# Five groups' second products in seven parts instead of eight, and planned steps handed out twice per block

## The chip, the cores and the metric

The kernel runs on one core of a Trainium2 chip. A core has TensorE (PE in the rows; PEld is its weight load), VectorE (DVE), ScalarE (ACT), GpSimd (POOL) and SyncE (SP, whose queue issues transfers), and 16 DMA engines. The metric is the device time of one execution in microseconds; the time of a kernel is the median of its runs.

## The reference

With x of 2048 rows by 512 columns, and six vectors of 512 from `silu(c) @ w_mod`:

```
h = layernorm(x) * (1 + ca) + sa
x = x + ga * Real(DFT_seq(DFT_hidden(h)))
h = layernorm(x) * (1 + cb) + sb
x = x + gb * ((silu(h @ w1) * (h @ w3)) @ w2)
```

w1 and w3 are 512 x 1792, w2 is 1792 x 512, all in float32. This case is about the last line.

## The kernel before

**Precision.** Every factor of a product is kept as a high part (a rounded copy, made by ScalarE's `copy`) and a low part (what is left, made by VectorE's `minus`). `product` (its matmuls are on L100) issues three matmuls: high by high, high by low, low by high. A matmul is 128 x 128 by 128 x 512. In the rows `hf` holds the two parts of the hidden values, `w2h` and `w2l` those of a weight, and `w1s`, `w1sh`, `w1sl` sums of weight blocks and their parts.

**Tiles.** The 1792 hidden columns are 7 groups g of 2 x 128, the 2048 rows are 4 blocks t of 512, the 512 columns are 4 blocks d of 128. Buffers are 50 slots of 128 x 2 x 512 float32; `take` and `give` hand them out in turn. Results of a matmul go to 8 banks.

**First groups.** `up(0, 0)`, `up(1, 0)`, eight units `down` for t = 0, then `up(0, 2)`, `up(1, 2)`. `up` runs four blocks (`up_block`) of twelve matmuls: w1 and w3, for q = 0 and 1. Blocks rotate over banks 0 to 3, `down` over banks 4 to 7. Rows of t = 2 (`h2h`, `h2l`) come from the layer norm of that block, which is a list of small steps (`ln2`, `chunk_parts`).

**Later groups.** For `items`, first the groups 2 to 6 of pair 0 (t = 0, 2) and then the groups 0 to 6 of pair 1 (t = 1, 3), the first products are made in Strassen's form: seven units `factor` in place of eight, written a1 to a7 for w1 and b1 to b7 for w3, each six matmuls. After most of them VectorE adds the bank to an earlier one (`plus`, L93) and, for w3, multiplies by the silu (`times`, L96); the others are copied by ScalarE. The order is written out by hand: a head `-b7 a1 a2 -b4 -b3` (a minus means the group before) and a body `a6 a5 y a7 y y a4 y a3 y b1 y b2 y b6 b5 y`. A `y` is one `down_unit` of the group before: six matmuls into one of banks 6 and 7 in turn, for one t and one d; ScalarE scales the bank into half a `y` tile (L335), and after two units GpSimd's queue adds the tile to `sums` in DRAM (L1146). Eight units serve one group. For the last two groups of pair 1, VectorE adds the bank to rows in SBUF instead.

**Steps handed out.** Work that prepares later operands stands in two lists: `background` (layer norm steps) and `jobs` (weights: high parts, for w1 and w3 also sums of blocks in four small operations, low parts, high and low parts of the sums). After each unit `beside` credits VectorE and ScalarE with the unit's length less what the unit itself uses of them, and `advance` issues steps from a list while there is credit. A step may push the credit below zero; then its engine must earn it back. A pause in the list ends a call. `jobs` go first; once they are empty the credit is cut to 1.0 and `background` goes on. `drain` issues whatever is still missing when a unit needs it. Each engine executes its instructions in the order in which they were issued. `behind(n, fn)` puts a step at the start of the n-th unit from there, ahead of that unit's own steps; `delayed` runs them.

Of the kernel before, what the change touches and what calls it, by code (L numbers as in the profile page):

```python
# [15 lines left out]
P = 128  # L16
# [26 lines left out]
def folded(nc, pools, c, cp, wmr, wmc, x, xt, ctr, cti, wdr, wdi, w1, w3, w2, out):  # L43
# [42 lines left out]
    def copy(dst, src, scale=1.0):  # L86
        nc.scalar.activation(dst, src, AF.Copy, scale=scale)  # L87

    def minus(dst, a, b):
        nc.vector.tensor_tensor(out=dst, in0=a, in1=b, op=OP.subtract)  # L90
# [4 lines left out]
    def times(dst, a, b):  # L95
        nc.vector.tensor_tensor(out=dst, in0=a, in1=b, op=OP.mult)  # L96
# [966 lines left out]
    def behind(units, fn):  # L1063
        if units:
            later.setdefault(units, []).append(fn)
        else:
            fn()
# [5 lines left out]
            later[n - 1] = later.pop(n)  # L1073


    def up_block(g, t, q, w):
        if q == 0 and w == "w1":
            drain(lambda: ("h2", t, 1) in done)
        to = bank(turn[0] % 4)
        turn[0] += 1  # L1080
        for d in range(ND):
            at = slice(d * P, (d + 1) * P)
            product(
                to,
                [u[:, q, at] for u in wuse[w, g]],
                [u[t, d // 2][:, d % 2, :] for u in (h2h, h2l)],
                d == 0,
                d == ND - 1,
            )
        if t == PAIRS[0][1] and q == 1:  # L1090
            give_w((w, g))
        if w == "w1":
            cur["v"] = take(F32, "v")
            nc.scalar.activation(cur["v"][:, 0, :], to, AF.Silu)
        else:
            v = cur.pop("v")
            times(v[:, 1, :], v[:, 0, :], to)
            u = hf[g, t, q] = take(F32R, "hf")
            copy(u[:, 0, :], v[:, 1, :])
            behind(1, lambda: minus(u[:, 1, :], v[:, 1, :], u[:, 0, :].bitcast(F32)))  # L1100
            behind(1, lambda: give(v))
# [106 lines left out]
    TO = {1: 0, 6: 0, 7: 0, 4: 0, 2: 1, 5: 2, 3: 2}  # L1208
    state, vs = {}, {}

    def right(pair, n):
        t0, t1 = PAIRS[pair]
        if n in (1, 2, 3):
            at = {1: (t0, 0), 2: (t0, 1), 3: (t1, 1)}[n]
            return h2h[at], h2l[at]
        at = pair, {5: 1, 6: 2, 7: 3, 4: 4}[n]
        return th[at], tl[at]

    def result(i, w, q, k, src):

        g, pair = items[i]
        v = vs[i][q][:, k, :]
        if w == "w1":
            behind(k != 0 or q == 0, lambda: nc.scalar.activation(v, src, AF.Silu))  # L1224
            return
        times(v, v, src)

        def highs():
            hf[g, PAIRS[pair][k], q] = take(F32R, "hf")
            copy(hf[g, PAIRS[pair][k], q][:, 0, :], v)  # L1230

        def lows():
            u = hf[g, PAIRS[pair][k], q]
            minus(u[:, 1, :], v, u[:, 0, :].bitcast(F32))

        behind(1, highs)
        behind(2, lows)

    def factor(i, w, n):
        g, pair = items[i]  # L1240
        key = (w, g, pair)
        st = state.setdefault((i, w), {})
        new = n in (1, 2, 5)
        if new:
            st[TO[n]] = bank(TO[n] + (0 if w == "w1" else 3))
        to = st[TO[n]]
        names = ("h", "l") if LEFT[n][0] == "h" else ("sh", "sl")
        for d in range(2):
            at = slice(int(LEFT[n][1]) * HALF + d * P, int(LEFT[n][1]) * HALF + (d + 1) * P)
            product(  # L1250
                to,
                [flat(wuse[key][x])[:, at] for x in names],
                [x[:, d, :] for x in right(pair, n)],
                new and d == 0,
                d == 1,
                not new,
            )
        if n == 1:
            st["x"] = take(F32, "x")
            if w == "w1":  # L1260
                vs[i] = [take(F32, "v") for _ in range(2)]
        if n == 5:
            st["y"] = take(F32, "x")
        if n in (1, 5, 6):
            copy(st["y" if n == 5 else "x"][:, n // 6, :], to)
        elif n == 4:
            result(i, w, 1, 0, to)
        else:

            own = st["y" if n == 7 else "x"][:, n % 2 if n < 7 else 0, :]  # L1270
            q, k = {2: (0, 0), 3: (0, 1), 7: (1, 1)}[n]
            dst = vs[i][q][:, k, :] if w == "w1" else own
            plus(dst, to, own)
            result(i, w, q, k, dst)
            if n == 7:
                behind(1, lambda: give(st["y"]))
        if n == 3:
            for x in wuse.pop(key).values():
                give(x)
            behind(1, lambda: give(st["x"]))  # L1280
            if w == "w3":
                for x in vs.pop(i):
                    behind(3, lambda x=x: give(x))


    loads.extend((n, m) for n in range(len(steps)) for m in range(2))
# [277 lines left out]
    FACTOR["b"].update({6: (0.0, 0.5), 7: (1.8, 0.5)})  # L1564

    def beside(us, used):
        advance(us - used[0], us - used[1], jobs)
        if not jobs:
            advance(0.0, 0.0)

    def up(g, t):
        for q in range(2):
            for w in ("w1", "w3"):
                drain(lambda: ((w, g), "l") in done, jobs)
                delayed()
                up_block(g, t, q, w)
                beside(2.72, USED[w])

    def down(g, pair, t, d, key):
        drain(lambda: (key, "l") in done, jobs)  # L1580
        delayed()
        down_unit(g, pair, t, d, key)
        beside(1.36, USED["own" if pair == 1 and g >= NG - 2 else "y"])

    for w in ("w1", "w3"):
# [35 lines left out]
    def unit(kind, i, n):  # L1621
        g, pair = items[i]
        more = i + 1 < len(items)
        if n == 1:
            drain(lambda: ("ready", i, "w1" if kind == "a" else "w3") in done, jobs)
        if (kind, i, n) == ("a", 0, 6):
            drain(lambda: ("t", 0, 4) in done)
        if (kind, i, n) == ("a", turning, 1):
            drain(lambda: not background)
        if kind == "a" and i == turning and n in (4, 5, 6, 7):  # L1630
            drain(lambda: ("t", 1, {6: 2, 5: 1, 7: 3, 4: 4}[n]) in done, jobs)
        delayed()
        factor(i, "w1" if kind == "a" else "w3", n)
        if (kind, n) == ("a", 1) and more:
            load_w(("w1", *items[i + 1]))
        if (kind, n) == ("a", 6):
            load_w(("w2", g, pair))
        if (kind, n) == ("a", 3) and more:
            load_w(("w3", *items[i + 1]))
            weight_jobs(i + 1, "w1")  # L1640
        if (kind, n) == ("b", 2):
            plain_jobs(("w2", g, pair))
        if (kind, n) == ("b", 3):
            if i + 2 == turning:
# [8 lines left out]
            for t in PAIRS[pair]:  # L1653
                seconds.extend((g, pair, t, d, ("w2", g, pair)) for d in range(ND))
        beside(1.36, FACTOR[kind][n])

    weight_jobs(0, "w3")
# [1 line left out]
    ln2(3)  # L1659
    for i in range(len(items)):  # L1660
        body = "a6 a5 y a7 y y a4 y a3 y b1 y b2 y b6 b5 y"
        if i == turning:
            body = "y y y y y a6 y a5 y a7 y b1 b2 a4 b6 a3 b5"
        if i == len(items) - 1:
            body = "a6 a5 y a7 y y a4 y a3 b1 y b2 b6 b5 y b7 y b4 y b3 y y y y y y y y"
        head = "-b7 a1 -b4 -b3 a2 " if i == turning else "-b7 a1 a2 -b4 -b3 " if i else "a1 a2 "
        for at in (head + body).split():
            if at == "y":
                if (i, len(seconds)) == (len(items) - 1, 4):
                    tc.mark_branch_hint_location("general", hint="LikelyTaken")  # L1670
# [809 lines left out]
```

## Time and profile before

| | |
|---|---|
| median of 3 runs | 707.81 us (705.94 to 708.52) |
| the profiled execution | 708.46 us, its span 706.7 us |
| mean granted TensorE clock | 0.991 |
| DMA traffic | 108.93 MB, mean 154 GB/s |
| accumulations `sum<-y` | 48 of 512 KB, 5.6 us from issue to landing |
| groups of pair 1 | from about 500 us to the end |

A row of the time order has its start and its duration in us, engine, line, operation, what it writes and reads, how many were merged, and in brackets the idle time before it and what ended that. Durations of neighbours on one engine overlap a little, so what a step costs in a full queue is the distance of two starts. A row of the windows has the stretch, its length, the busy time of each engine (with instructions), the granted clock, the share of the DMA engines, and GB/s.

### The profile page before, as it was taken

What the parts mean: (1) busy time and instruction counts of PE and PEld (TensorE: products, weight loads), DVE (VectorE), ACT (ScalarE), POOL (GpSimd) and SP (SyncE); (2) the same over time, 40 slices, a digit from 0 to 9 for tenths busy, and PEclk for the clock granted to TensorE, in tenths of its full rate; (3) what the DMA queues carried; (4) which work ended last, traced back from release to release, by engine and by line L of the source; (5) the groups of instructions that cost most, each with busy time, mean ns of one, the idle gap of its engine ahead of it and who ended that gap; (6) DMA issues with size and microseconds to landing.
All of it is one profiled execution on the core that took longest, in us unless ns stands there. A gap on an engine that the chain in (4) does not pass through costs nothing.

```text
span 706.7 us, 8912 instructions
## 1 busy us (share of the span) xinstructions
PE 686.3 (97%) x3152; PEld 564.7 (80%) x3152; DVE 548.3 (78%) x877; ACT 430.8 (61%) x709; POOL 119.4 (17%) x141
## 2 busy tenths in 40 slices
PE   7999999999999999899999999999999999999995
PEld 4898888888888888687888788787788888888784
DVE  5999679997999978579987886896865556664763
ACT  4998865545454655745677676867665565656420
POOL 1320253542524000200100101011010100101000
PEclk9999999999999999999999999999999999999998
DMA  8730299796678521522868558376763847537403
GB/s 266 211 120 1 77 373 328 251 307 229 207 283 287 168 86 41 92 58 64 209 114 199 89 130 153 61 156 137 239 136 73 180 62 175 111 69 162 137 0 124
DMA packets 38100, 108.93 MB, mean 154 GB/s; under 512 B 4896, under 2 KB 5152, under 8 KB 38048
## 3 DMA queue, kind: packets, MB, share of 16 engines
q0 software_dynamic: 12352, 43.00, 29.3%
q1 hardware_dynamic: 25264, 63.98, 27.5%
q10 hardware_dynamic: 432, 1.31, 0.5%
q8 instruction: 26, 0.43, 0.3%
q14 instruction: 26, 0.21, 0.1%
HBM read 76.81 MB, written 33.55 MB: 156 GB/s over the span
## 4 chain that ended last, share of the span: by engine, by line
PE 81%; DVE 7%; ACT 6%; issue 2%; DMA 2%; SPq 1%; ACTq 0%; DVEq 0%
PE bank L100 52%; PE bank L750 25%; PE bank L559 2%; PE bank L598 1%; DMA wmr<-in_wmr 1%; ACT xc L894 1%; PE bank L576 1%; DVE xc L96 1%; SPq L231 1%; ACT hf L87 1%; ACT y L335 1%; DVE v L96 0%; DVE hl L90 0%; ACT hm L501 0%; DMA w<-in_wdi 0%
## 5 line engine op out<-in xcount | busy, mean ns | idle before, releaser
L100 PE MATMUL bank<-hf,w2h 128*128 128x512 f32 (+1 forms) x452 | 140.9, 391 | 0.3
L1146 POOL DMA_DIRECT2D sum<-y x48 | 41.0, 855 | 390.1 <-ACT y L335 373.0
L100 PEld LDWEIGHTS bank<-hf,w2h 128*128 128x128 f32 x452 | 84.3, 188 | 22.1 <-DVE hf L90 3.4
L100 PE MATMUL bank<-hf,w2l 128*128 128x512 f32 (+1 forms) x226 | 87.6, 388 | 0.0
L87 ACT ACTIVATE hf<-v 128x512 fp32r<-128x512 f32 x56 | 35.3, 630 | 67.3 <-DVE v L96 62.7
L335 ACT ACTIVATE y<-bank,gb 128x512 f32<-128x512 f32 x96 | 64.9, 682 | 18.6 <-PE bank L100 18.3
L93 DVE TENSOR_TENSOR v<-bank,x 128x512 f32<-128x512 f32 x36 | 24.7, 685 | 34.9 <-PE bank L100 34.8
L750 PE MATMUL bank<-bh,us 128*128 128x512 f32 x128 | 49.9, 390 | 0.0
L93 DVE TENSOR_TENSOR x<-bank,x 128x512 f32<-128x512 f32 x36 | 24.7, 687 | 32.4 <-PE bank L100 28.7
L750 PE MATMUL bank<-bh,ul 128*128 128x512 f32 x128 | 49.8, 389 | 0.0
L750 PE MATMUL bank<-d,us 128*128 128x512 f32 x128 | 49.8, 389 | 0.0
L750 PE MATMUL bank<-d,uh 128*128 128x512 f32 x128 | 49.8, 389 | 0.0
L750 PE MATMUL bank<-l,us 128*128 128x512 f32 x128 | 49.8, 389 | 0.0
L750 PE MATMUL bank<-l,uh 128*128 128x512 f32 x128 | 49.8, 389 | 0.0
L100 PEld LDWEIGHTS bank<-hf,w2l 128*128 128x128 f32 x226 | 42.4, 188 | 8.4
L90 DVE TENSOR_TENSOR hf<-v,hf 128x512 fp32r<-128x512 f32 x56 | 38.5, 687 | 12.2 <-ACT hf L87 12.1
L170 POOL DMA_INDIRECT re<-in_ctr,mirror x32 | 35.8, 1117 | 66.2 <-DVE ul L90 39.5
L1224 ACT ACTIVATE v<-v 128x512 f32<-128x512 f32 x36 | 22.8, 632 | 38.8 <-DVE v L93 38.8
L87 ACT ACTIVATE x<-bank 128x512 f32<-128x512 f32 x72 | 41.4, 586 | 7.2 <-PE bank L100 6.5
L170 POOL DMA_INDIRECT im<-in_cti,mirror x32 | 32.7, 1023 | 35.3 <-PE bank L750 10.0
L100 PE MATMUL bank<-h2h,w1h 128*128 128x512 f32 x80 | 31.8, 397 | 1.5 <-ACT h2h L87 1.5
L100 PE MATMUL bank<-h2l,w1h 128*128 128x512 f32 x80 | 31.9, 399 | 0.8 <-DVE h2l L90 0.8
(246 smaller groups left out, 1775.2 us busy)
## 6 DMA issues: line engine op xcount, KB each, us to landing
sum<-y POOLq DMA_DIRECT2D x48, 512.0 KB, 5.6
w<-in_w SPq DMA_DIRECT2D x42, 512.0 KB, 4.5
re<-in_ctr SPq DMA_DIRECT2D x32, 256.0 KB, 5.0
im<-in_cti SPq DMA_DIRECT2D x32, 256.0 KB, 5.0
wmc<-in_wmc SPq DMA_DIRECT2D x8, 512.0 KB, 6.3
xr<-in_xt SPq DMA_DIRECT2D x8, 512.0 KB, 7.6
sum<-xr SPq DMA_DIRECT2D x8, 512.0 KB, 6.2
x<-in_x SPq DMA_DIRECT2D x11, 256.0 KB, 4.8
```

The source lines that it names most:

```text
L87: nc.scalar.activation(dst, src, AF.Copy, scale=scale)
L90: nc.vector.tensor_tensor(out=dst, in0=a, in1=b, op=OP.subtract)
L93: nc.vector.tensor_tensor(out=dst, in0=a, in1=b, op=OP.add)
L96: nc.vector.tensor_tensor(out=dst, in0=a, in1=b, op=OP.mult)
L100: nc.tensor.matmul(acc, lhs[a], rhs[b], start=first and n == 0, stop=last and n == len(PASSES) - 1, skip_group_check=more,)
L170: nc.gpsimd.indirect_dma_start(dst, None, rows, bass.IndirectOffsetOnAxis(ap=at, axis=0))
L231: queue.dma_start(raw_w[dt][q * 64 : (q + 1) * 64, m, :], w[i][par::2, q])
L335: nc.scalar.activation(dst, src, AF.Identity, scale=by)
L559: nc.tensor.matmul(halves(hb[k])[:, m, :], sides((hh, hl)[a][k])[:, dt, m, :], wu[dt][:, b, m, :], start=False, stop=dt % 2 == 1 and n == ...
L750: nc.tensor.matmul(acc[what, e], lhs, rhs, start=begin and i == 0, stop=(end or (turn and what == "x")) and i == len(terms) - 1, skip_grou ...
L1146: nc.gpsimd.dma_start(sums[t, d // 2], y, accum_op=OP.add)
L1224: behind(k != 0 or q == 0, lambda: nc.scalar.activation(v, src, AF.Silu))
```

## The change

For the groups 0 to 4 of pair 1 (`SEVEN`) the second product too is made in Strassen's form: seven units of six matmuls instead of eight. The right factors are the four blocks of hidden values and three sums of them (four `minus` steps), each with a high and a low part, handed out by `behind` after the unit b3 whose result is the last of the four. The left factors are the blocks of w2 and four sums of them, prepared by five steps in `jobs` instead of two. A unit goes to both banks 6 and 7, three matmuls each; products 3, 6, 7 and 4 add to what the unit before left in the banks, and after every unit ScalarE copies both banks into a tile, which GpSimd's queue adds to `sums`. The bodies behind these groups have seven `y` in place of eight: one of the two between a7 and a4 is gone.

Besides, `up_block` is cut into two halves of six matmuls with a `beside` behind each, and as long as the rows of t = 2 are not ready, and w3 of group 1 has been begun, `background` goes before `jobs`.

```diff
-    def up_block(g, t, q, w):
+    def up_block(g, t, q, w, part):
...
-        to = bank(turn[0] % 4)
-        turn[0] += 1
-        for d in range(ND):
+        if part == 0:
+            cur["to"] = bank(turn[0] % 4)
+            turn[0] += 1
+        to = cur["to"]
+        for d in range(2 * part, 2 * part + 2):
...
+        if part == 0:
+            return
...
+    SEVEN = [(g, 1) for g in range(NG - 2)]
+    ORDER7 = (2, 5, 3, 1, 6, 7, 4)
+    LEFT7 = {1: "h0", 2: "h2", 4: "h3", 5: "s0", 6: "s1", 7: "s2", 3: "s3"}
+    TO7 = {2: (0, 0), 5: (1, 1), 3: (0, 1), 1: (0, 0), 6: (0, 1), 7: (1, 1), 4: (1, 0)}
+    right7, banks7 = {}, []
...
         times(v, v, src)
+        if (g, pair) in SEVEN:
+            seven_parts(i, q, k)
+            return
...
+    def seven_parts(i, q, k):
+        key = items[i]
+        v = {(a, b): vs[i][a][:, b, :] for a in range(2) for b in range(2)}
+
+        def high(n, src):
+            right7[key, n] = take(F32R, "hf")
+            copy(right7[key, n][:, 0, :], src)
+
+        def low(n, src):
+            u = right7[key, n]
+            minus(u[:, 1, :], src, u[:, 0, :].bitcast(F32))
+
+        if (q, k) != (0, 1):
+            n = {(0, 0): 1, (1, 0): 2, (1, 1): 3}[q, k]
+            behind(1, lambda: high(n, v[q, k]))
+            behind(2, lambda: low(n, v[q, k]))
+            return
+        t1, t2, t3, t4 = v[0, 0], v[1, 1], v[0, 1], v[1, 0]
+        behind(1, lambda: minus(t1, v[0, 1], v[0, 0]))
+        behind(1, lambda: minus(t3, v[1, 1], v[0, 1]))
+        behind(2, lambda: high(5, t1))
+        behind(2, lambda: minus(t2, v[1, 1], t1))
+        behind(2, lambda: high(7, t3))
+        behind(3, lambda: low(5, t1))
+        behind(3, lambda: minus(t4, v[1, 0], t2))
+        behind(3, lambda: high(6, t2))
+        behind(4, lambda: low(6, t2))
+        behind(4, lambda: high(4, t4))
+        behind(5, lambda: low(7, t3))
+        behind(6, lambda: low(4, t4))
+
+    def seven_jobs(key):
...
+        step(jobs, 1, highs, 0.0, 1.0)
+        step(jobs, 1, totals, 1.4)
+        step(jobs, 1, lows, 1.2)
+        step(jobs, 1, sum_highs, 0.0, 1.0)
+        step(jobs, 1, sum_lows, 1.2)
+
+    def seven_unit(g, pair, n, key):
+        new = n in (1, 2, 5)
+        if new:
+            banks7[:] = [bank(6), bank(7)]
+        y = take(F32, "y")
+        which, k = TO7[n]
+        t = PAIRS[pair][k]
+        names = ("h", "l") if LEFT7[n][0] == "h" else ("sh", "sl")
+        u = right7.pop(((g, pair), n))
+        for e, to in enumerate(banks7):
+            at = int(LEFT7[n][1]) * HALF + e * P
+            product(
+                to,
+                [flat(wuse[key][x])[:, at : at + P] for x in names],
+                [u[:, b, :] for b in range(2)],
+                new,
+                True,
+                not new,
+            )
+            d = 2 * which + e
+            copy_by(y[:, e, :], to, gb[:, d : d + 1])
+        give(u)
+        nc.gpsimd.dma_start(sums[t, which], y, accum_op=OP.add)
+        behind(4, lambda: give(y))
...
-                    behind(3, lambda x=x: give(x))
+                    behind(7 if items[i] in SEVEN else 3, lambda x=x: give(x))
...
     def beside(us, used):
-        advance(us - used[0], us - used[1], jobs)
-        if not jobs:
-            advance(0.0, 0.0)
+        early = ("h2", PAIRS[0][1], 1) not in done and ("w3", 1) in wuse
+        first, second = (background, jobs) if early else (jobs, background)
+        advance(us - used[0], us - used[1], first)
+        if early or not first:
+            advance(0.0, 0.0, second)
...
-                up_block(g, t, q, w)
-                beside(2.72, USED[w])
+                for part in range(2):
+                    up_block(g, t, q, w, part)
+                    beside(1.36, USED[w] if part else (0.0, 0.0))
...
-            plain_jobs(("w2", g, pair))
+            (seven_jobs if (g, pair) in SEVEN else plain_jobs)(("w2", g, pair))
...
+        if i and items[i - 1] in SEVEN:
+            body = "a6 a5 y a7 y a4 y a3 y b1 y b2 y b6 b5 y"
```

The four operations of `totals` in `seven_jobs` are those of `weight_jobs` with other blocks.

More of the change, by code (lines that the diff above doesn't have):

```diff
@@ L1073, in delayed @@
             later[n - 1] = later.pop(n)
-    def up_block(g, t, q, w):
-        if q == 0 and w == "w1":
+    def up_block(g, t, q, w, part):
+        if q == 0 and w == "w1" and part == 0:
             drain(lambda: ("h2", t, 1) in done)
-        to = bank(turn[0] % 4)
-        turn[0] += 1
-        for d in range(ND):
+        if part == 0:
[3 more added lines that the diff above has]
+        for d in range(2 * part, 2 * part + 2):
             at = slice(d * P, (d + 1) * P)
@@ new lines, in seven_jobs, with highs, totals, lows @@
+    def seven_jobs(key):
+        use = wuse[key] = {}
+        def highs():
+            use["h"] = take(F32R, "w2h")
+            copy(flat(use["h"]), flat(wraw[key]))
+        def totals():
+            use["s"] = take(F32, "w2s")
+            s, r = four(use["s"]), four(wraw[key])
+            plus(s[:, 0, :], r[:, 1, :], r[:, 3, :])
+            minus(s[:, 1, :], s[:, 0, :], r[:, 0, :])
+            minus(s[:, 2, :], r[:, 0, :], r[:, 1, :])
+            minus(s[:, 3, :], r[:, 2, :], s[:, 1, :])
+        def lows():
+            use["l"] = take(F32R, "w2l")
+            r = wraw.pop(key)
+            minus(flat(use["l"]), flat(r), flat(use["h"]).bitcast(F32))
+            give(r)
+        def sum_highs():
+            use["sh"] = take(F32R, "w2sh")
+            copy(flat(use["sh"]), flat(use["s"]))
+        def sum_lows():
+            use["sl"] = take(F32R, "w2sl")
+            minus(flat(use["sl"]), flat(use["s"]), flat(use["sh"]).bitcast(F32))
+            give(use.pop("s"))
+            done.add((key, "l"))
+        step(jobs, 1, highs, 0.0, 1.0)
[3 more added lines that the diff above has]
+        step(jobs, 1, sum_lows, 1.2)
@@ new lines, in seven_unit @@
+    def seven_unit(g, pair, n, key):
[22 more added lines that the diff above has]
+        behind(4, lambda: give(y))
+        if n == ORDER7[-1]:
+            for x in wuse.pop(key).values():
+                give(x)
+            if g == NG - 3:
+                for t in PAIRS[pair]:
+                    load_sums(t)
@@ L1575, in up, with down @@
                 delayed()
-                up_block(g, t, q, w)
-                beside(2.72, USED[w])
-    def down(g, pair, t, d, key):
+                for part in range(2):
+                    up_block(g, t, q, w, part)
+                    beside(1.36, USED[w] if part else (0.0, 0.0))
+    def down(g, pair, *which):
+        key = which[-1]
         drain(lambda: (key, "l") in done, jobs)
         delayed()
-        down_unit(g, pair, t, d, key)
+        if (g, pair) in SEVEN:
+            seven_unit(g, pair, *which)
+        else:
+            down_unit(g, pair, *which)
         beside(1.36, USED["own" if pair == 1 and g >= NG - 2 else "y"])
@@ L1652, in unit @@
                 weight_jobs(i + 1, "w3")
-            for t in PAIRS[pair]:
-                seconds.extend((g, pair, t, d, ("w2", g, pair)) for d in range(ND))
+            if (g, pair) in SEVEN:
+                seconds.extend((g, pair, n, ("w2", g, pair)) for n in ORDER7)
+            else:
+                for t in PAIRS[pair]:
+                    seconds.extend((g, pair, t, d, ("w2", g, pair)) for d in range(ND))
         beside(1.36, FACTOR[kind][n])
```

## The prediction

> **What bounds the kernel now.** I read the page first, then the chain that ended last, then stage windows, then single engines in order of time.
>
> ```profile
> span 706.7 us, 8912 instructions
> PE 686.3 (97%) x3152; PEld 564.7 (80%) x3152; DVE 548.3 (78%) x877; ACT 430.8 (61%) x709; POOL 119.4 (17%) x141
> ```
>
> TensorE is busy 97% of the span, so removing matmuls is worth their issue time, as long as nobody makes TensorE wait. From the chain:
>
> ```profile
> 88.22 174.32 PE bank L750 x768
> ```
>
> 768 matmuls in 174.32 us: 0.227 us each, and 1.36 us for a unit of six. The next view is the windows (duration; then busy us of PE, PEld, DVE, ACT, POOL; clock; DMA share; GB/s). The first row is one whole second-half group, from one a6 to the next; the second its first 7 us.
>
> ```profile
> 538.77:568.93 30.16, 30.16 (x133) 24.70 (x132) 17.85 (x27) 18.24 (x28) 3.40 (x4) 1.00 0.59 122
> 538.97:545.93 6.96, 6.96 (x31) 5.48 (x30) 6.89 (x11) 4.18 (x6) 0.00 (x0) 1.00 0.01 2
> ```
>
> A group is 132 matmuls, 29.96 us, and takes 30.16. VectorE is busy 59% of it on average, but 99% of the stretch that begins when -b3 ends. The change puts most of its new VectorE work into that stretch, so the average says little here.
>
> **Part 1, 30 matmuls fewer.** Seven units of six in place of eight, in five groups: 5 x 6 x 0.227 = 6.8 us, or 1.36 a group.
>
> **Part 2, what VectorE must do first.** This is its queue at the head of a group (start, duration):
>
> ```profile
> 538.97 0.69 DVE L93 TENSOR_TENSOR x<-bank,x 128x512 f32<-128x512 f32 x1 [0.67 <-PE bank L100]
> 539.69 0.69 DVE L96 TENSOR_TENSOR v<-v,x 128x512 f32<-128x512 f32 x1
> 540.30 0.42 DVE L93 TENSOR_TENSOR w3s<-w 128x256 f32<-128x256 f32 x1
> ...
> 541.77 0.68 DVE L90 TENSOR_TENSOR hf<-v,hf 128x512 fp32r<-128x512 f32 x1
> 542.37 1.22 DVE L90 TENSOR_TENSOR w3l<-w,w3h 128x1024 fp32r<-128x1024 f32 x1
> 543.51 0.68 DVE L90 TENSOR_TENSOR hf<-v,hf 128x512 fp32r<-128x512 f32 x1
> 544.11 1.22 DVE L90 TENSOR_TENSOR w3sl<-w3s,w3sh 128x1024 fp32r<-128x1024 f32 x1
> 545.24 0.68 DVE L93 TENSOR_TENSOR v<-bank,x 128x512 f32<-128x512 f32 x1
> ```
>
> Start to start, a 128x512 step costs 0.60 to 0.61 us (0.72 when the next one reads it), the four w3 totals 1.47, a 128x1024 split 1.13 to 1.14. The w3 steps are handed out with -b3, a6 and a5, and stay there: the credits at -b3 depend only on the stated costs, which the change leaves alone. In their order the steps after the change are: sum and product of -b3, totals (to 541.77), low part 2 (ends 542.46, as now), t1 (starts 542.37), t3 (542.98), w3l (543.59), t2 (544.73), w3sl (545.34), low part 5 (546.47, ends 547.16), t4 (547.07), low part 6 (547.68), then the sum of a7 (548.28, ends 548.97; today it starts at 545.24). Low 7 and low 4 follow and are early enough.
>
> What TensorE meets there, before:
>
> ```profile
> 541.49 0.62 PE L100 MATMUL bank<-hf,w2h 128*128 128x512 f32 x2
> ...
> 542.17 0.84 PE L100 MATMUL bank<-hf,w2h 128*128 128x512 f32 x2
> 542.84 0.39 PE L100 MATMUL bank<-hf,w2l 128*128 128x512 f32 x1
> ```
>
> The pair at 542.17 ends at 543.01, so its second matmul began at 542.62 instead of 542.40: it waited 0.22 us for the low part that ended at 542.46. So an operand is used 0.16 us after VectorE ends it. And what a restart costs:
>
> ```profile
> 449.89 0.39 PE L100 MATMUL bank<-hf,w2l 128*128 128x512 f32 x1
> 450.76 0.50 PE L100 MATMUL bank<-th,w1sh 128*128 128x512 f32 x1 [0.48 <-ACT x L87]
> 451.10 0.39 PE L100 MATMUL bank<-tl,w1sh 128*128 128x512 f32 x1
> ```
>
> After a gap the next step is 0.34 us instead of 0.23: 0.11 more per stop.
>
> First y unit (product 2). Its second matmul already reads low part 2 (today the fifth does): due 541.72, ready 542.62, a wait of 0.90 plus 0.11. It ends at 543.87; 0.79 more than today. a7 runs to 545.23.
>
> Second y unit (product 5). Its second matmul reads low part 5: ready 547.16 + 0.16 = 547.32. Its first must wait for ScalarE too, since every y unit now uses both banks 6 and 7. ScalarE's rows give the price of its steps:
>
> ```profile
> 542.90 0.58 ACT L87 ACTIVATE x<-bank 128x512 f32<-128x512 f32 x1
> 543.38 0.68 ACT L335 ACTIVATE y<-bank,gb 128x512 f32<-128x512 f32 x1
> 545.96 0.63 ACT L1224 ACTIVATE v<-v 128x512 f32<-128x512 f32 x1 [1.90 <-DVE v L93]
> 546.50 0.67 ACT L335 ACTIVATE y<-bank,gb 128x512 f32<-128x512 f32 x1
> ```
>
> High part 6 stands ahead of the two copies of the first y unit and needs t2 (ends 545.42): 545.46 plus the 0.54 of such a step (545.96 to 546.50) is 546.00, the first copy ends at 546.68. So TensorE idles 545.23 to 546.75, does one matmul, waits again to 547.32, and ends the unit at 548.57 (0.34 and four steps, and 0.23): 1.98 late.
>
> a4 adds into the bank that the sum of a7 reads, with one y unit between them instead of two: 548.97 and about 0.1 (no more than the 0.16 above) make 549.07, 0.50 after it could start, with the restart 0.61. Behind it the third y unit is due at 550.54; bank 6 is free at 550.22 (silu of a7 from 549.01, then the copy), so no wait. From a3 on the new steps (two copies a unit, w2's four totals and its second split) fit: w2's end near 564.5, and VectorE's next sum is due at 565.6.
>
> Waits 0.79 + 1.98 + 0.61 = 3.38 against 1.36 saved: **+2.0 a group, +10.1 for five**. Bounds: below, only the first wait (0.79), should w3's steps come behind low part 5; above, 3.38 plus a low clock (a rival).
>
> **Part 3, before the first of the five.** Group (0, 1)'s w2 has five steps instead of two in front of w1's:
>
> ```profile
> 496.08 0.69 DVE L93 TENSOR_TENSOR x<-bank,x 128x512 f32<-128x512 f32 x1 [3.39 <-PE bank L100]
> ...
> 497.42 1.22 DVE L90 TENSOR_TENSOR w2l<-w,w2h 128x1024 fp32r<-128x1024 f32 x1
> 498.56 0.68 DVE L90 TENSOR_TENSOR hf<-v,hf 128x512 fp32r<-128x512 f32 x1
> 500.09 0.69 DVE L93 TENSOR_TENSOR v<-bank,x 128x512 f32<-128x512 f32 x1 [0.85 <-PE bank L100]
> ...
> 502.17 1.22 DVE L90 TENSOR_TENSOR w1l<-w,w1h 128x1024 fp32r<-128x1024 f32 x1
> ```
> ```profile
> 503.44 0.50 PE L100 MATMUL bank<-h2h,w1l 128*128 128x512 f32 x1 [0.21 <-DVE w1l L90]
> ```
>
> Totals from 497.42 to 498.89, split to 500.03, low part to 500.63, second split to 501.77: the sum that starts at 500.09 starts 1.7 us later, w1l ends 505.1 instead of 503.39, and TensorE already waits for it. **+1.8**, once; bounds 0 (should w2's new steps be handed out after w1's) and 2.0 with a restart.
>
> **Part 4, half blocks.** Here TensorE waits for h2 of t = 2 (second view: ScalarE; third: windows):
>
> ```profile
> 294.80 0.39 PE L100 MATMUL bank<-hf,w2l 128*128 128x512 f32 x1
> 296.71 0.51 PE L100 MATMUL bank<-h2h,w1h 128*128 128x512 f32 x1 [1.53 <-ACT h2h L87]
> 297.97 0.79 PE L100 MATMUL bank<-h2l,w1h 128*128 128x512 f32 x1 [0.76 <-DVE h2l L90]
> ...
> 301.03 0.39 PE L100 MATMUL bank<-h2h,w1l 128*128 128x512 f32 x1
> ```
> ```profile
> 295.61 1.05 ACT L87 ACTIVATE h2h<-xc 128x1024 fp32r<-128x1024 f32 x1
> ...
> 297.13 1.05 ACT L87 ACTIVATE h2h<-xc 128x1024 fp32r<-128x1024 f32 x1
> ```
> ```profile
> 295.03:301.03 6.00, 3.72 (x9) 2.63 (x9) 3.65 (x8) 4.43 (x6) 1.89 (x3) 0.72 1.04 180
> 284.14:295.03 10.89, 10.89 (x49) 8.82 (x47) 5.49 (x11) 8.49 (x13) 1.85 (x2) 1.00 0.40 55
> ```
>
> From 295.03 (294.80 and 0.23) to 301.03 eight matmuls went, worth 1.82: 4.2 us lost, 2.3 idle and 1.9 at a lower clock. The two h2h steps come with the seventh and eighth y unit. After the change, by the planner's stated costs: from -1.1 of VectorE credit (the last row step gives 5.0, its three steps of 5.2 start from -0.9), eight blocks give 8 x 2.72 less 4 x 1.2, hence 15.9, plus 1.36 a y unit; ahead of the last low part stand 14.4 (t = 2's own) and 4.8 (four weight splits), 19.2. So it is handed out with the third y unit, five units (6.8 us) before it is needed. What is late next is w2's split for g = 1, moved behind it to the second y unit and needed by the fifth: hidden. The square root and its table load fall between blocks, where four banks rotate. **-4.2**; bounds 0 and -4.2.
>
> The same lateness shows once more:
>
> ```profile
> 323.50 0.39 PE L100 MATMUL bank<-h2h,w1l 128*128 128x512 f32 x1
> 324.11 0.50 PE L100 MATMUL bank<-th,w1sh 128*128 128x512 f32 x1 [0.23 <-ACT x L87]
> ```
>
> 0.61 + 0.34 instead of 0.45: **-0.4** of at most 0.5, as the th steps ahead of ScalarE's copy move forward too. What else moves with ln2(1) and ln2(3) I bound by stops like that at 450.76, three at 0.75: 2.3 us either way, taken as zero.
>
> **Part 5, transfers.** Seven accumulations a group instead of four, each on POOL's queue, on which nothing else stands:
>
> ```profile
> 547.46 0.85 POOL L1146 DMA_DIRECT2D sum<-y  x1 [13.46 <-ACT y L335]
> ```
>
> The share 0.59 of 30.16 is 17.8 us of DMA a group; charged wholly to the four accumulations, seven take 31.1, inside the 32.2 that a group will last. Weights are asked for eleven units (15 us) ahead on SP's queue. Cost zero.
>
> **The sum.** +10.1 + 1.8 - 4.2 - 0.4 = +7.3 us. The profiled execution took 708.46 (its span 706.7 and 1.8 around it), so 715.8; the median of the runs stands 0.65 lower, so **715**.
>
> **Rivals.**
> - *Faster: VectorE's order does not bind the second y unit.* If low part 5 ended by 545.2, 2.0 us earlier than I count (w3's two splits, 2.27 us, behind it), only the first wait stays: 5 x (0.79 - 1.36) + 1.8 - 4.6 = -5.7, or 702. For it: the new VectorE steps of a group (seven of 0.60, the totals 1.47, a split 1.14) are 6.8 us, ScalarE's (six copies of 0.57, three high parts of 0.54, a weight step of 0.95) 6.0 us; with 17.85 and 18.24 both stay under 25 of 28.6. Against it: the rows show both splits inside the stretch, and VectorE's order is the program's. 0.19.
> - *Slower still: the clock falls at each head.* The window row above shows 0.72 after 1.53 and 0.76 us of idling; the stop of 0.48 did not do it. The new heads idle 0.9, 1.5, 0.3 and 0.5 us within 8, between the two. At the price of that row (1.9 at low clock), less the 0.4 or so of a4's wait that it would cover, 5 x 1.5 = +7.5: 722.5. 0.13. The Trainium skill ("TensorE: Matmul & The Clock Gate", section "What's actually happening") has the clock fall only after an idle window of about 3.4 us; by that rule it stays full here and the time is 715. The trace does not agree with it as worded: two pauses, 2.3 us in all, were enough.
> - *The half blocks do nothing at 295* (a step earlier in the list waits for its engine): +4.6, 719.7. For it speaks ScalarE, 8.49 of 10.89 us busy in the second window row; against it, that its long steps (square root, table load) leave that stretch. 0.05.
> - *The parts cancel*, at half the waits of the heads: +10.1 becomes 5 x (1.69 - 1.36) = +1.7, the time 706.7. 0.05.
>
> **How the numbers follow.** My forecast has 0.58; its own range, with the 2.3 us either way and 0.5 us a group, is 710 to 720. Half a per cent, 3.5 us, is about what a measurement of this kernel tells from no change. Faster 0.19, within 0.07 (the last rival and the foot of my own range, under 711.3), slower 0.74. A range from 703 to 721 leaves out about half of the first rival and most of the second.
>
> **What would show it.** Right: each of five heads has TensorE stops of about 0.9, 1.5 and 0.5 us whose releasers are VectorE's hf, ScalarE's y and VectorE's v; the cycle from a6 to a6 is 32.2 us; VectorE is busy without a pause for 11 us from the end of -b3; the first matmul with t = 2's h2 follows the last y unit at once, clock 1.00. Wrong: cycles of 28.6 to 29.4 us with w3l behind low part 5 in VectorE's order, or a clock under 1.00 in the heads.

## The result

The changed kernel takes 723.23 us (median of 6 runs, 722.07 to 729.44) against 707.65 us before on the same chip (705.94 to 709.93): ratio 1.0227, 95% interval 1.0205 to 1.0249, or 15.6 us slower. The forecast was 715, its range 703 to 721. The profiled execution took 722.07 us. From its page, the span and the engines:

```profile
span 720.3 us, 8993 instructions
PE 684.4 (95%) x3122; PEld 559.0 (78%) x3122; DVE 583.3 (81%) x937; ACT 459.3 (64%) x759; POOL 131.6 (18%) x156
```

There are 30 matmuls fewer, as there should be, yet TensorE's busy time fell by only 1.9 us, not 6.8: busy time grows with a low clock, and each restart adds to it. VectorE has 35 us more work. The list of TensorE's waits (total us, times, longest us) shows who it waited for:

```profile
PE bank L100 <- ACT y L335: 9.2, 7, 1.5
PE bank L100 <- DVE hf L90: 3.2, 5, 0.6
PE bank L100 <- DVE w2l L90: 2.6, 1, 2.6
...
PE bank L100 <- DVE w1l L90: 1.9, 1, 1.9
PE bank L100 <- DVE v L93: 1.9, 5, 0.4
...
PE bank L100 <- ACT x L87: 1.3, 1, 1.3
```

Five of each of the entries with five or seven times are the heads of the five groups. The other two of the seven (1.22 and 0.43 us) and the entries with one are single stops in the groups before them.

**Where the time went, in four stretches.** The same matmuls in both kernels serve as marks: the first with h2, the first of the first a6, the one that waits for `w1l` before the first of the five groups, and the first of that group's first y unit. Before (the rows at 324.11 and 503.44 stand in the prediction):

```profile
262.38 0.39 PE L100 MATMUL bank<-h2h,w1h 128*128 128x512 f32 x1
...
511.32 0.62 PE L100 MATMUL bank<-hf,w2h 128*128 128x512 f32 x2
```

After:

```profile
261.48 0.39 PE L100 MATMUL bank<-h2h,w1h 128*128 128x512 f32 x1
...
326.81 0.50 PE L100 MATMUL bank<-th,w1sh 128*128 128x512 f32 x1 [1.33 <-ACT x L87]
...
505.34 0.50 PE L100 MATMUL bank<-h2h,w1l 128*128 128x512 f32 x1 [1.87 <-DVE w1l L90]
...
514.81 0.39 PE L100 MATMUL bank<-hf,w2h 128*128 128x512 f32 x1
```

| stretch | before | after | difference |
|---|---|---|---|
| start to the first matmul with h2 | 262.38 | 261.48 | -0.9 (code left alone: no effect of the change) |
| from there to the first a6 | 61.73 | 65.33 | +3.6 |
| to the `w1l` matmul (its stop included) | 179.33 | 178.53 | -0.8 |
| to the first y unit of the first head | 7.88 | 9.47 | +1.6 |
| to the end: five groups and the tail | 195.38 | 205.49 | +10.1 |

The sum is 13.6 us, the difference of the spans. The stop at 505.34 grew by 1.65 us (after 503.09 the next matmul came 2.25 us later, where the trace of before has 0.60). So the third stretch without it is -2.45, and before the first head +3.2 us are lost.

**The heads.** One of the five, TensorE's rows at its stops:

```profile
548.10 0.50 PE L100 MATMUL bank<-hf,w2h 128*128 128x512 f32 x1 [0.64 <-DVE hf L90]
...
552.40 1.00 PE L100 MATMUL bank<-hf,w2sh 128*128 128x512 f32 x2 [1.52 <-ACT y L335]
...
554.71 0.50 PE L100 MATMUL bank<-th,w1h 128*128 128x512 f32 x1 [0.38 <-DVE v L93]
```

VectorE's rows of the same head, and ScalarE's:

```profile
549.29 1.22 DVE L90 TENSOR_TENSOR w3l<-w,w3h 128x1024 fp32r<-128x1024 f32 x1
550.42 0.69 DVE L90 TENSOR_TENSOR v<-v,v 128x512 f32<-128x512 f32 x1
551.03 1.22 DVE L90 TENSOR_TENSOR w3sl<-w3s,w3sh 128x1024 fp32r<-128x1024 f32 x1
552.16 0.69 DVE L90 TENSOR_TENSOR hf<-v,hf 128x512 fp32r<-128x512 f32 x1
...
553.96 0.69 DVE L93 TENSOR_TENSOR v<-bank,x 128x512 f32<-128x512 f32 x1
```
```profile
551.14 0.63 ACT L87 ACTIVATE hf<-v 128x512 fp32r<-128x512 f32 x1 [0.62 <-DVE v L90]
551.68 1.25 ACT L335 ACTIVATE y<-bank,gb 128x512 f32<-128x512 f32 x2
```

VectorE splits w3 twice (549.29 and 551.03) before it comes to low part 5 (552.16). High part 6 (551.14) waits for its difference, which lies between the two splits; the copies of the first y unit stand behind it on ScalarE (551.68), and the second y unit cannot start until the first of them has emptied its bank: 1.52 us. Then the sum of a7 (553.96) is late, and a4 waits for it.

The windows show one whole cycle, its head, the stretch before the first head, and the one in the first groups:

```profile
548.10:580.35 32.25, 29.72 (x126) 23.41 (x126) 24.73 (x40) 23.98 (x38) 5.95 (x7) 1.00 0.79 163
548.30:555.30 7.00, 5.10 (x20) 3.34 (x20) 6.96 (x11) 5.06 (x10) 0.85 (x1) 1.00 0.15 9
505.34:510.01 4.67, 4.67 (x13) 3.67 (x14) 3.67 (x5) 1.37 (x3) 0.00 (x0) 0.64 0.39 155
...
290.06:298.56 8.50, 5.89 (x15) 4.35 (x15) 7.47 (x7) 4.74 (x7) 1.86 (x2) 0.60 0.81 162
```

A cycle holds 126 matmuls, worth 28.6 us, and lasts 32.25. At the head VectorE is busy 99% of the time, the clock full. In the last two rows it is not: 0.64 after the stop of 1.87 us, and 0.60 around the two stops that follow.

**The first groups.** TensorE's two stops in the y units between `up(1, 0)` and `up(0, 2)`:

```profile
290.06 0.73 PE L100 MATMUL bank<-hf,w2h 128*128 128x512 f32 x2 [1.22 <-ACT y L335]
293.40 0.79 PE L100 MATMUL bank<-hf,w2l 128*128 128x512 f32 x1 [2.61 <-DVE w2l L90]
```

What VectorE and ScalarE did there:

```profile
288.06 0.69 DVE L90 TENSOR_TENSOR hf<-v,hf 128x512 fp32r<-128x512 f32 x1 [1.22 <-ACT hf L87]
290.99 1.23 DVE L90 TENSOR_TENSOR h2l<-xc,h2h 128x1024 fp32r<-128x1024 f32 x1 [2.24 <-ACT h2h L87]
292.13 1.22 DVE L90 TENSOR_TENSOR w2l<-w,w2h 128x1024 fp32r<-128x1024 f32 x1
```
```profile
282.61 0.63 ACT L87 ACTIVATE hf<-v 128x512 fp32r<-128x512 f32 x1 [2.70 <-DVE v L96]
283.14 1.04 ACT L87 ACTIVATE w2h<-w 128x1024 fp32r<-128x1024 f32 x1
284.20 1.28 ACT L1098 ACT_TABLE_LOAD   x1
285.50 0.60 ACT L1098 ACTIVATE v<-bank 128x512 f32<-128x512 f32 x1
285.99 1.51 ACT L894 ACTIVATE xc<-xc,sb,cb 128x512 f32<-128x512 f32 x2
287.40 0.62 ACT L87 ACTIVATE hf<-v 128x512 fp32r<-128x512 f32 x1
287.93 1.51 ACT L894 ACTIVATE xc<-xc,sb,cb 128x512 f32<-128x512 f32 x2
289.34 0.67 ACT L335 ACTIVATE y<-bank,gb 128x512 f32<-128x512 f32 x1
289.91 1.05 ACT L87 ACTIVATE h2h<-xc 128x1024 fp32r<-128x1024 f32 x1
```

w2's high part was ready at 284.18, but its low part stands on VectorE behind `h2l`, which waits 2.24 us for ScalarE's `h2h`. ScalarE is itself late: it waited 2.70 us for VectorE's product, loaded the table back for the last silu, and the first y copy, whose unit ended at about 284.6 (283.24 and 1.36), starts at 289.34. After its wait ScalarE works without a pause: a weight step, the table load, the silu and four layer norm steps (`xc`, 3.0 us) stand ahead of that copy. VectorE in turn waits 1.22 and 2.24 us for ScalarE's results, so each engine stands in order behind a step of the other.

### The profile page after: what moved, and what is told of

The parts are those of the page before. It is cut to its first block, busy times and chain, and to the rows that moved or that the text cites. A ratio compares the mean times of both kernels' runs of the same rounds, so it can differ in the third digit from the quotient of the medians.

```text
span 720.3 us, 8993 instructions
## 1 busy us (share of the span) xinstructions
PE 684.4 (95%) x3122; PEld 559.0 (78%) x3122; DVE 583.3 (81%) x937; ACT 459.3 (64%) x759; POOL 131.6 (18%) x156
## 4 chain that ended last, share of the span: by engine, by line
PE 73%; DVE 17%; ACT 6%; issue 2%; DMA 1%; POOL 0%; SPq 0%; ACTq 0%; DVEq 0%
PE bank L100 45%; PE bank L750 24%; DVE hf L90 2%; DVE v L90 2%; PE bank L559 1%; DVE v L96 1%; PE bank L598 1%; DVE xr L805 1%; DVE w3l L90 1%; DVE w3sl L90 1%; DVE w3s L90 1%; ACT hm L501 1%; DMA x<-in_x 1%; ACT hf L87 1%; DVE x L93 1%
## 5 line engine op out<-in xcount | busy, mean ns | idle before, releaser
L100 PE MATMUL bank<-hf,w2h 128*128 128x512 f32 (+1 forms) x352 | 111.9, 397 | 5.0 <-DVE hf L90 3.2
L87 ACT ACTIVATE hf<-v 128x512 fp32r<-128x512 f32 x71 | 44.8, 632 | 80.8 <-DVE v L96 66.3
L335 ACT ACTIVATE y<-bank,gb 128x512 f32<-128x512 f32 x126 | 82.6, 684 | 15.3 <-PE bank L100 14.6
L100 PEld LDWEIGHTS bank<-hf,w2h 128*128 128x128 f32 x352 | 66.5, 191 | 23.8 <-DVE hf L90 6.3
L100 PE MATMUL bank<-hf,w2l 128*128 128x512 f32 (+1 forms) x176 | 69.3, 394 | 2.6 <-DVE w2l L90 2.6
L1150 POOL DMA_DIRECT2D sum<-y x28 | 24.0, 857 | 248.7 <-ACT y L335 238.1
L90 DVE TENSOR_TENSOR hf<-v,hf 128x512 fp32r<-128x512 f32 x71 | 48.4, 688 | 13.0 <-ACT hf L87 12.7
L1342 POOL DMA_DIRECT2D sum<-y x35 | 29.8, 851 | 143.4 <-ACT y L335 123.4
L100 PEld LDWEIGHTS bank<-hf,w2l 128*128 128x128 f32 x176 | 33.7, 191 | 9.8 <-DVE w2l L90 3.0
L100 PE MATMUL bank<-hf,w2sh 128*128 128x512 f32 x80 | 26.6, 404 | 7.6 <-ACT y L335 7.6
```

What stands on the lines that cost most here:

```text
L100: nc.tensor.matmul(acc, lhs[a], rhs[b], start=first and n == 0, stop=last and n == len(PASSES) - 1, skip_group_check=more,)
L335: nc.scalar.activation(dst, src, AF.Identity, scale=by)
L1150: nc.gpsimd.dma_start(sums[t, d // 2], y, accum_op=OP.add)
L1342: nc.gpsimd.dma_start(sums[t, which], y, accum_op=OP.add)
```

## Experiments

All edits are to the changed kernel. Each was timed beside the kernel before on its own chip; there its medians were 709.8 to 710.6 us. All kernels compute the whole reference.

**The two halves of the change apart.** First the seven products alone:

```diff
-        early = ("h2", PAIRS[0][1], 1) not in done and ("w3", 1) in wuse
+        early = False
...
-                    beside(1.36, USED[w] if part else (0.0, 0.0))
+                beside(2.72, USED[w])
```

> The seven products alone; blocks and their steps as in the kernel before. Theory (VectorE's order at five heads costs 3.4 us each against 1.36 saved, and w1 is 1.8 us late once, with about 1.4 us of low clock behind it): 707.7 + 10.2 + 3.2 = about 721. Rival (the half blocks carry half of the loss, as their two new stops at 290 and 293 us suggest): about 715 to 717.

Measured: 722.87 us against 709.77, ratio 1.0173 (1.0147 to 1.0200), +13.1 us where the theory had +13.4. Then the half blocks alone:

```diff
-    SEVEN = [(g, 1) for g in range(NG - 2)]
+    SEVEN = []
```

> The half blocks alone; second products in eight units as before. As predicted at first: 703. Theory from the new trace (4.2 us won at the first w1 matmul of t = 2 and up to 2.5 us later, lost again to waits for w2's split of group 1, a low clock and a late copy): 708, no difference. Rival (they carry half of the loss): 714.

Measured: 711.66 against 709.77, ratio 1.0019 (1.0003 to 1.0035), +1.9 us (0.2 to 2.5 by the interval) where the prediction had -4.6. The two sum to +15.0, the change itself to +15.6: within the intervals they do not interact. The seven products are what makes the kernel slow, and the half blocks, counted as a gain, are a small loss. Their two parts, steps handed out twice per block and `background` ahead of `jobs`, were not run apart.

**VectorE's order at the heads.** The five w3 steps are queued when a7 is issued, not at -b3, so that they come behind the parts of the hidden values:

```diff
+        if (kind, n) == ("a", 7) and i and items[i - 1] in SEVEN:
+            weight_jobs(i, "w3")
...
-            if more:
+            if more and items[i] not in SEVEN:
                 weight_jobs(i + 1, "w3")
```

> The changed kernel, with w3's five steps in the five heads handed out behind a7 instead of behind -b3, so that they stand behind low part 5. Theory (VectorE's order): the heads' stops of 0.9, 1.9 and 0.5 us all go, 5 x 3.4 = 17 us, to 706. Rival (both banks and ScalarE's copies hold the second y unit): only the first stop goes, 719.

Measured: 711.00, ratio 1.0026 (1.0010 to 1.0043). Of its cycles and its heads:

```profile
518.88:548.46 29.58, 29.16 (x126) 23.50 (x126) 24.90 (x40) 23.18 (x38) 5.98 (x7) 1.00 0.85 178
```
```profile
518.88 0.73 PE L100 MATMUL bank<-hf,w2sh 128*128 128x512 f32 x2 [0.31 <-ACT y L335]
```

The cycle falls from 32.25 to 29.58 us, 13.4 us over five groups, with VectorE's work unchanged (24.90 and 24.73 us busy). No VectorE stop is left in the heads, so the order of these steps was most of the cost. The 17 us of the theory were not reached (12.2 by the medians): a ScalarE stop of 0.31 us remains in each head. The edit moves w3's two ScalarE steps along with the three of VectorE; that its high part was not the cause shows further down, where it goes back to -b3 and no stop returns.

**ScalarE's order and the banks as the rival cause.** High part 6 goes behind the copies of the first y unit:

```diff
-        behind(3, lambda: high(6, t2))
-        behind(4, lambda: low(6, t2))
+        behind(4, lambda: high(6, t2))
+        behind(5, lambda: low(6, t2))
```

> The changed kernel, with high part 6 one unit later (low part 6 too), so that ScalarE's two copies of the first y unit no longer stand behind it. Theory (low part 5 is ready no sooner): the first matmul of the second y unit starts early, its second still waits, no difference, 723. Rival (the copies and the two banks set the stop): 5 x 1.5 us less, 716.

Measured: 723.53, ratio 1.0186 (1.0135 to 1.0237): no gain beyond the intervals. In TensorE's rows the first matmul of the second y unit now waits 0.27 us instead of 1.52, but the second waits for low part 5; and after it the clock fell in two of the five heads, of which this is the first:

```profile
551.50 0.50 PE L100 MATMUL bank<-hf,w2sh 128*128 128x512 f32 x1 [0.27 <-ACT y L335]
553.25 0.50 PE L100 MATMUL bank<-hf,w2sh 128*128 128x512 f32 x1 [1.25 <-DVE hf L90]
```
```profile
554.98:557.11 2.13, 2.13 (x6) 1.67 (x5) 1.22 (x3) 1.23 (x3) 0.60 (x1) 0.50 0.90 175
```

The wait moved from ScalarE's copy to VectorE's low part, as it must if VectorE's order sets the end. Cycles were 31.7 us where the clock stayed full (a4's wait is gone, since low 6 now stands behind the sum of a7) and 33.2 where it fell.

**The stop before the first head.** At the turn from pair 0 to pair 1, w1's steps are queued at b1, ahead of w2's five (queued at b2), instead of behind them at a3:

```diff
+            if i != turning:
+                weight_jobs(i + 1, "w1")
+        if (kind, n) == ("b", 1) and i == turning:
             weight_jobs(i + 1, "w1")
```

> The changed kernel, with w1's five steps for the first group behind the turn handed out with b1, ahead of w2's five, instead of with a3. Theory (w2's three new steps push w1's split back, and the stop lowers the clock): the stop of 1.9 us at 505 and the low clock behind it go, about 3.4 us less than the changed kernel. Rival (the clock fell for another reason, or the stop moves to w2's split): 2 us less or nothing.

Measured: 720.88, ratio 1.0151 (1.0129 to 1.0174).

```profile
504.34 0.39 PE L100 MATMUL bank<-h2h,w1l 128*128 128x512 f32 x1
```
```profile
516.58 0.74 PE L100 MATMUL bank<-hf,w2sh 128*128 128x512 f32 x2 [1.65 <-ACT y L335]
519.68 0.50 PE L100 MATMUL bank<-th,w1h 128*128 128x512 f32 x1 [1.44 <-DVE v L93]
```

The `w1l` matmul runs without a stop and no low clock follows. The first head then stops differently (1.65 and 1.44 us, without the first of the three). Against the ratio of the changed kernel the gain is 0.76%, 5.4 us where 3.4 was expected; each of the two ratios has an interval of 0.22% (1.6 us) either way. From the first matmul with h2 (at 263.13 here) to the end of the span the two profiles differ by 3.35 us, near the 3.2 that the stretch had lost. That is a sum of several differences, though: besides the first head, the clock fell behind one later head (0.67 from 583 to 588 us), whose cycle took 33.2 us.

**The split of w2 in the first groups.** Weights go first again once the y units begin:

```diff
-        early = ("h2", PAIRS[0][1], 1) not in done and ("w3", 1) in wuse
+        early = ("h2", PAIRS[0][1], 1) not in done and ("w3", 1) in wuse and not turn[1]
```

> The changed kernel, with the weight list first again from the first y unit on, so that w2's split of group 1 goes ahead of the last two low parts of t = 2. Theory (that order alone makes the stop of 2.6 us at 293 and the low clock behind it): both go, about 4.5 us less than the changed kernel, and t = 2 is still ready in time. Rival (the steps are too many for these blocks): the stop moves to t = 2's low parts, no gain.

Measured: 723.78, ratio 1.0191 (1.0167 to 1.0214). The stop of 2.61 us is gone, so the order of the lists made it. But there are two new ones, of 0.52 us in a1 (320.78) and 2.00 us in a2 of the first group of `items`, and the stop at the first a6, which the changed kernel has too (1.33), stays:

```profile
323.98 0.50 PE L100 MATMUL bank<-h2h,w1h 128*128 128x512 f32 x1 [2.00 <-DVE v L96]
327.18 0.79 PE L100 MATMUL bank<-th,w1sh 128*128 128x512 f32 x1 [1.37 <-ACT x L87]
```

After the stop at a6 the clock fell to half for 4.9 us (327.18 to 332.04, matmuls 0.43 apart). The expected gain was handed back 30 us later. So the missing split was one of several stops of the same kind: steps moved ahead by credit leave others late, and taking away one uncovers the next.

**All four edits together, with and without the half blocks.**

> The changed kernel with four edits: w3's steps behind a7, high part 6 one unit later, w1 sooner at the turn, the weight list first from the first y unit on. Theory: the stops found so far go, 723.2 - 13.4 - 2.0 - 3.3 - 4.5 = 700 where before is 707.7, about 1.1% faster than before. Rival (new stops take their place): 705 or more.

> The same without the half blocks: blocks and lists as in the kernel before, with the seven products and the first three edits. Theory: 3 to 4 us more than with all four, about 703.5, as the wait for t = 2 and its low clock are back. Rival (the half blocks give nothing even so): equal.

Measured: 707.91, ratio 0.9964 (0.9945 to 0.9983), and without the half blocks 706.67, ratio 0.9942 (0.9925 to 0.9959). Both are a little faster than the kernel before (0.4 and 0.6%, beyond the intervals), but short of the 700 and 703.5 expected: both rivals came true. New stops took the place of old ones (in the first kernel 0.43, 2.00 and 0.40 us at 320 to 327 us, and one in each head), and the half blocks bring nothing here either. Each head of the second kernel still stops once, too. ScalarE's rows there, and TensorE's:

```profile
575.26 1.07 ACT L87 ACTIVATE w3h<-w 128x1024 fp32r<-128x1024 f32 x1
576.21 0.64 ACT L1234 ACTIVATE v<-v 128x512 f32<-128x512 f32 x1
576.73 1.27 ACT L335 ACTIVATE y<-bank,gb 128x512 f32<-128x512 f32 x2
```
```profile
577.47 0.73 PE L100 MATMUL bank<-hf,w2sh 128*128 128x512 f32 x2 [0.63 <-ACT y L335]
```

w3's high part, moved along with the rest of w3, now stands ahead of the y copies on ScalarE (0.95 us, 575.26 to 576.21).

**w3's high part back at -b3**, the other four steps behind a7:

```diff
-                weight_jobs(i + 1, "w3")
+                weight_jobs(i + 1, "w3", (True, items[i] not in SEVEN))
...
+            weight_jobs(i, "w3", (False, True))
```

> The kernel of the last expectation (whole blocks, seven products, three edits), with w3's high part handed out with -b3 again and only its other four steps behind a7. Theory: its heads still lose about 1.0 us each because ScalarE makes w3's high part (0.95) just ahead of the copy that the third y unit waits for; that goes, 5 x 0.9 = 4.5 us less, to 0.988 of the kernel before. Rival (ScalarE is simply full in that stretch): the stop moves, 0.994 again.

Measured: 703.08 against 709.83, ratio 0.9902 (0.9887 to 0.9918). One cycle of it:

```profile
552.14:581.10 28.96, 28.96 (x127) 23.45 (x127) 24.83 (x40) 23.29 (x38) 5.97 (x7) 1.00 0.87 183
```

28.96 us for 126 matmuls and the first of the next cycle; TensorE has no idle time in it, and the 30.16 of the kernel before shrank by 1.2 of the 1.36 that six matmuls are worth. VectorE is as busy as in the changed kernel (24.83 and 24.73 us). ScalarE's order was thus the second limit, worth 0.64 us a cycle (29.60 to 28.96; 3.2 for five, where 4.5 was expected), and it showed only when VectorE's was out of the way.

**Half blocks only while they are wanted**: until the rows of t = 2 are ready, with weights first in the y units.

```diff
+                halved = ("h2", PAIRS[0][1], 1) not in done
+                if halved:
+                    beside(1.36, (0.0, 0.0))
...
+                beside(1.36 if halved else 2.72, USED[w])
```

> The same, with the half blocks in force only until t = 2's rows are ready, and the weight list first from the first y unit on. Theory (the late stops at 320 to 327 us come from steps handed out twice per block after t = 2 is ready): t = 2's wait and its low clock go without new stops, 3 to 4 us less than with whole blocks. Rival (the list, once moved forward, collides with w1's and w3's steps however it goes on): no gain over whole blocks.

Measured: 700.31 against 709.83, ratio 0.9866 (0.9848 to 0.9884): 9.5 us faster than the kernel before and, by the two ratios (0.9866 and 1.0227), about 26 faster than the change as made. In its first groups two stops are left: 1.23 us for the same y copy of ScalarE at 292.92, and 0.69 us at the first a6 (323.99).

With h2 ready in time and w2's split not moved behind it, the half blocks do give a part of what they were to give: 2.8 us by the medians.

## Why the prediction was right or wrong

**Part 1 and Part 2 (heads): right in mechanism and size.** Forecast +10.1 us for five groups; the stretch from the first head to the end grew by 10.1, and the cycles are 32.25 to 32.29 us where 32.2 was said. The three stops have the releasers named (hf, y, v). That even the tenth agrees is luck. By the starts of its matmuls TensorE comes out of the three stops 0.68, 2.08 and 0.66 us later than with eight units, where 0.79, 1.98 and 0.61 were forecast. The first was too long because the prediction's 0.16 and 0.11 us price one delay twice: in the trace of before, too, the matmul behind the waiting one starts 0.38 us after VectorE's end (542.46 to 542.84), not 0.50. And the cycles alone give 5 x 2.1 = 10.5, of which the stretch behind the last head gives 0.4 back. The mechanism was tested from both sides: moving w3's steps took 2.67 us off each cycle (that the 29.58 left is the prediction's lower bound, 30.16 + 0.79 - 1.36 = 29.6, is chance: the first wait, which the bound kept, went, and one of ScalarE came); moving ScalarE's step, with VectorE's order as it was, only changed the name of the wait. The rival that VectorE's order does not bind is refuted by the rows 549.29 to 552.16.

**The rival of a low clock at each head did not come** in the changed kernel: 1.00 in the heads. It did come in two heads of five once two of the stops stood close together (0.27 and 1.25 us within 1.8), and in one head of five in each of two kernels whose heads stop just as in the changed kernel (0.63 and 1.51 us): with w1 sooner at the turn and with weights first in the y units. There the clock was 0.67 over 5 us, and the cycle took 33.2 us instead of 32.25. So the full clock in all five heads of the changed kernel was in part luck; the rival was a real one, at 1.0 to 1.6 us a head where it priced 1.5.

**Part 3: right mechanism, term too small.** The stop grew by 1.65 us (forecast 1.8), but the clock fell behind it: 13 matmuls in 4.67 us instead of 2.95. The part cost 3.2 us by the table, outside its bounds of 0 to 2.0. The prediction asked about the clock at the heads only and not at this stop, the longest of all that it forecast.

**Part 4: the step that failed, and the reason for the miss.** Forecast -4.2 and -0.4. Alone it measured +1.9; in the profile +3.6 up to the first a6. One piece was right: the rows of t = 2 came early enough, and no matmul with h2 waited. The sentence that failed is that w2's split, moved behind them to the second y unit and needed by the fifth, is hidden. It was handed out there, but executed at 292.13, because the credits count an engine's own work and not the waits of VectorE and ScalarE for each other. The place of the square root was named too, and its cost taken as hidden; the table load back for silu (284.20) now stands ahead of the last silu of `up(1, 0)` and so of the product that both engines wait for. That the order of the lists made the stop is shown by the run with weights first in the y units, where it is gone. With the y copy 1.22 us, w2's split 2.61, and a low clock for the twelve matmuls behind it, the stretch lost more than the 4.2 us that it was to save. The bounds of this part, 0 and -4.2, left no room for a loss. The second saving turned round as well: at the first a6 the stop grew from 0.23 to 1.33 us. Its releaser is the same ScalarE copy as before, so the copy is later still; which of the steps moved ahead of it delays it was not tested.

The rival "the half blocks do nothing" was nearest, and still too mild. Other ln2 shifts, taken as zero within 2.3 us either way, came to -2.45: the stops of the kernel before at 389.32, 450.76 and 455.43 vanish. It is the half blocks' doing as well: with them alone the same three are gone, with the seven products alone they stay. This is why the half blocks' loss of 3.6 us shrank to about 1.2 by the time 500 us in, within the interval of the measured 1.9.

**Part 5: right.** No stop of TensorE in the feed-forward stage has a transfer as its releaser, and one accumulation takes 5.9 us to land instead of 5.6.

**The sum.** From the profile: +10.1, +3.2 and +1.15 (3.6 less 2.45) against +10.1, +1.8 and -4.6. Between the profiled executions the miss is 6.3 us (722.07 against 715.8): 5.8 in Part 4 and 1.4 in Part 3, less 0.9 in the stages ahead. The medians lie 2 us further apart than these two executions; where that comes from the single traces do not show.

## What to carry to other kernels

A saved matmul is worth its time only if the engines that prepare operands have their steps in the right order: here an engine with 25 us of work in a cycle of 29 cost 2.67 us a cycle through the totals and splits of a weight that nobody needed yet, and the second limit (ScalarE's w3 step) came to light only when the first was gone. A step handed out early is not a step done early: follow it through the queue of its engine and of every engine that its predecessors wait for, and price what was passed by the time at which it will really run. Ask of every stop that a change adds, not only of the repeated ones, whether the clock may fall behind it.

## What the hardware showed

The clock after short stops did not follow their length alone. The kernel before, the kernel with the seven products alone, and the one with w3's high part back at -b3 (whole blocks, like the other two) meet the same two stops at the first matmuls with t = 2's h2 (1.53 us for `h2h`, then 0.75 or 0.76 for `h2l`). Their windows from the first of these matmuls on, in this order:

```profile
296.71:301.03 4.32, 3.56 (x8) 2.63 (x9) 3.63 (x8) 2.75 (x3) 1.03 (x2) 0.60 1.08 180
```
```profile
298.53:302.90 4.37, 3.62 (x10) 2.65 (x11) 3.61 (x8) 2.75 (x3) 1.03 (x2) 0.71 1.06 177
```
```profile
298.92:303.20 4.28, 3.52 (x14) 2.47 (x14) 3.41 (x7) 2.79 (x4) 1.03 (x2) 1.00 1.06 171
```

With the same stops the clock fell at once, after three matmuls, or not at all. The same holds for the heads with one program: with high part 6 later, two of five heads had the clock at 0.50 for about 2.1 us, and the other three, with the same stops to 0.02 us, did not. Two further kernels have one such head each among five with the same stops (clock 0.67 over 5 us, told above). The single stop of 1.87 us at 505.34 lowered it from 507.03 to 510.01. The Trainium skill ("TensorE: Matmul & The Clock Gate", section "What's actually happening") says that the window over which activity is counted runs free of the program, so that the same kernel varies with its phase. The rows agree with that, and with its two states (0.23 and 0.43 us between matmuls here). They do not agree with an idle window of about 3.4 us as the condition: no single stop in these rows was as long as that. What amount of idle time in a window decides, these runs don't settle; a stop of one to two microseconds is best priced as a chance of a further 1.0 to 2.5 us, which is what the falls in these traces cost.
